# State products and old states' part of y by head, in 64-wide tiles of TensorE's array, in a retention and SwiGLU kernel

## The chip, the cores and the metric

The kernel runs on one core of a Trainium2 chip. The metric is the device time of one execution in microseconds (us), as the median of several executions. A profile is one further look at one execution, with the start and length of each instruction. Its span, from the first to the last instruction, is about 2 us shorter than the time.

TensorE is the matmul engine: an array of 128 rows by 128 columns, which holds the weights (the stationary operand) while the columns of the moving operand stream through. Here it is used as one array or in tiles: two tiles of 64 columns side by side, two of 64 rows, or, in the change, the two tiles of 64 by 64 on the array's diagonal. VectorE, ScalarE and GpSimd work element by element. The profile calls these engines PE, DVE, ACT and POOL, PEld is TensorE's weight loading, and a trailing q (ACTq) marks an engine's sequencer.

## The reference, cut to what matters

```python
# retention: 4 batches, 8 heads, 768 steps, heads of 64
gamma = 1.0 - 2.0 ** (-5.0 - np.arange(H))
for t in range(S):
    state = gamma * state + einsum('bhd,bhe->bhde', k[:, :, t], v[:, :, t])
    y[:, :, t] = scale * einsum('bhd,bhde->bhe', q[:, :, t], state)
# ... y reshaped to x, 3072 tokens by 512, then the SwiGLU FFN
g = x @ w_gate;  val = x @ w_val
out = (g * sigmoid(g) * val) @ w_out
```

## The kernel before

Retention is done in chunks of 128 steps. For a chunk, "scores" multiplies k by q for each head, "mix" adds to y what the states of earlier chunks give and then what the chunk itself gives, and "state" updates the states. There are 8 heads of 64, so two heads fill the 128 partitions: a state tile holds four pairs of heads, and for each pair a block of 128 by 128 in which only the two diagonal 64 by 64 blocks are not zero. The zeros let one full-array matmul serve two heads.

```python
states = [consts.tile([P, NP, P], F32, name=f"state{i}") for i in range(4)]
for t in states:
    nc.gpsimd.memset(t, 0.0)
# ...
def state(c):
    # ... new[:, n] = old[:, n] * gdec, on ScalarE
    st = bank("st")
    for n in range(NP):
        nc.tensor.matmul(st[:, ts(n, P)], kd[:, ts(n, P)], vn[:, ts(n, P)], ...)
    for i in range(2):
        r = ds(D * i, D)
        if ci == 0:
            nc.scalar.copy(new[r, :, r], pairs(st)[r, :, r])
        else:
            nc.vector.tensor_tensor(new[r, :, r], new[r, :, r],
                                    pairs(st)[r, :, r], op=ALU.add)

def mix(c):
    # ...
    y = bank("y")
    if ci:
        prev = state_of(c, 1)
        for n in range(NP):                       # the old states' part
            nc.tensor.matmul(y[:, ts(n, P)], prev[:, n], qd[:, n], ...)
    for n in range(NP):                           # the part within the chunk
        for i in range(2):
            nc.tensor.matmul(y[ds(D * i, D), ts(n, P)], vn[:, ts(2 * n + i, D)],
                             a[i][:, n], ...)
    nc.scalar.copy(xT[:, :, c // NCK % 2, ts(ci % L, P)], pairs(y))
# ... in between: sums for the FFN, its weights' conversion on VectorE
# (tensor_scalar twice, then a merge of the signs) and GpSimd
```

The 24 chunks are spread over four segments of six. The first segment's retention is the start of the kernel, up to 42 us. The other three stand in between the matmuls of an FFN's second product, one or two retention blocks at a time; I call these the three retention stages. The FFN's first product follows each of them. The first one, right after the start, is the "up stage", and TensorE's matmuls of 384 columns belong to it.

Of the kernel before, what the change touches and what calls it, by code (L numbers as in the profile page):

```python
# [10 lines left out]
F32 = mybir.dt.float32  # L11
# [3 lines left out]
ALU = mybir.AluOpType  # L15

P = 128
B, H, S, D = 4, 8, 768, 64
NP = H // 2
# [22 lines left out]
def tile_retnet_swiglu(  # L42
# [37 lines left out]
    nc = tc.nc  # L80

    consts = ctx.enter_context(tc.tile_pool(name="consts", bufs=1))
# [16 lines left out]
    def bank(tag):  # L99

        own = {"x": (0, 1), "wz": (2, 3), "s": (4, 5), "st": (6,), "y": (7,)}[tag]
        turn[tag] = turn.get(tag, -1) + 1
        return banks[own[turn[tag] % len(own)]]
# [200 lines left out]
    gdec = tab[:, GDEC0:NTAB]  # L304



    states = [consts.tile([P, NP, P], F32, name=f"state{i}") for i in range(4)]
    for t in states:
        nc.gpsimd.memset(t, 0.0)  # L310
    xT = consts.tile([P, NC, 2, TH], F32, name="xT")
    xsa = consts.tile([P, 4, KH, TH], F32, name="xs")
    xs = [xsa[:, i] for i in range(4)]
# [5 lines left out]
    def pairs(t):  # L319
        return t.rearrange("p (n t) -> p n t", n=NP)  # L320

    def state_of(c, old=0):
        return states[2 * (c // NCK % 2) + (c + old) % 2]
# [24 lines left out]
    def state(c):  # L348
        ci = c % NCK
        if ci == NCK - 1:  # L350
            return
        vn, kd = chunks[c][2:]
        new, old = state_of(c), state_of(c, 1)
        if ci:
            for n in range(NP):
                nc.scalar.activation(new[:, n], old[:, n], AF.Copy,
                                     scale=gdec[:, ds(n, 1)])
        st = bank("st")
        for n in range(NP):
            nc.tensor.matmul(st[:, ts(n, P)], kd[:, ts(n, P)], vn[:, ts(n, P)],  # L360
                             start=(n == 0), stop=True, skip_group_check=True)
        for i in range(2):
            r = ds(D * i, D)
            if ci == 0:
                nc.scalar.copy(new[r, :, r], pairs(st)[r, :, r])
            else:
                nc.vector.tensor_tensor(new[r, :, r], new[r, :, r],
                                        pairs(st)[r, :, r], op=ALU.add)

    def mix(c):  # L370
        ci = c % NCK
        qd, vn = pairs(chunks[c][1]), chunks[c][2]
        a = att.pop(c)
        y = bank("y")
        if ci:
            prev = state_of(c, 1)
            for n in range(NP):
                nc.tensor.matmul(y[:, ts(n, P)], prev[:, n], qd[:, n],  # L378
                                 start=(n == 0), stop=False, skip_group_check=True)
        for n in range(NP):  # L380
            for i in range(2):
                nc.tensor.matmul(y[ds(D * i, D), ts(n, P)], vn[:, ts(2 * n + i, D)],  # L382
                                 a[i][:, n], start=(ci == 0 and n == 0), stop=True,
                                 skip_group_check=True)
        nc.scalar.copy(xT[:, :, c // NCK % 2, ts(ci % L, P)], pairs(y))  # L385

    def retention(s):



        cs = seg_chunks(s)

        def last(n):
            state(cs[n])
            del chunks[cs[n]]
            if s and n + 3 < len(cs):
                load_chunk(cs[n + 3], places_of(n))

        steps = [lambda: scores(cs[0])]
        for n, c in enumerate(cs):  # L400
            if n + 1 < len(cs):
                steps.append(lambda n=n: scores(cs[n + 1]))
            steps.append(lambda c=c: mix(c))
            steps.append(lambda n=n: last(n))
            if n % 2:
                steps.append(lambda n=n: sums_x(n // 2))
        return steps
# [447 lines left out]
```

## Time and profile before

| | before |
|---|---|
| time, median of 3 (range) | 746.63 us (745.86 to 747.22) |
| span of the profile | 744.2 us |
| first segment, to TensorE's second start | 0 to 41.97 us |
| from there to the last matmul of the up stage (384 columns) | 116.02 us |
| three retention stages | 78.07, 77.39 and 77.51 us |
| from the last matmul of 192 columns to the end | 57.46 us |

I measure a stage from the first second-product matmul after the FFN's first product to the next matmul of 192 columns (which only the later first products have). That takes in some FFN work which does not change, but both ends are sharp in the trace.

This view cuts the kernel before into stretches. Its columns are the stretch, its length, then busy time and number of instructions of PE, PEld, DVE, ACT and POOL, the granted TensorE clock, the DMA share and GB/s.

```profile
0.00:42.00 42.00, 29.20 (x277) 24.64 (x277) 26.58 (x41) 21.00 (x41) 18.88 (x20) 0.99 0.91 316
337.33:414.72 77.39, 77.39 (x522) 66.79 (x521) 41.43 (x77) 14.69 (x39) 9.47 (x8) 1.00 0.36 126
```

In the second row TensorE is busy all of the time and VectorE half of it: there only TensorE's own work counts. In the first row TensorE idles for 13 us and no engine is full, so waits decide.

### The profile page before, as it was taken

How to read it: one execution, taken by the hardware profiler on the slowest of the kernel's cores; microseconds unless marked ns; L12 is line 12 of the kernel's file. 1: busy time of each engine (PE TensorE's matmuls, PEld its weight loads, DVE VectorE, ACT ScalarE, POOL GpSimd, SP SyncE). 2: the span in 40 equal slices, each digit the busy share in tenths (PEclk: the TensorE clock that was granted, in tenths of full speed). 3: DMA queues.
4: the chain of work that ended last, by engine and by line, in shares of the span. 5: the costliest groups of instructions: out<-in, count | busy, mean ns of one | idle time of the engine just before them, and what ended most of it. 6: DMA issues, size and time to landing. Idle time of an engine off the chain costs nothing.

```text
span 744.2 us, 11024 instructions
## 1 busy us (share of the span) xinstructions
PE 720.2 (97%) x4196; PEld 625.5 (84%) x4196; DVE 489.1 (66%) x845; ACT 246.7 (33%) x488; POOL 246.2 (33%) x156
## 2 busy tenths in 40 slices
PE   6889999999999999999999999999999999999997
PEld 5745555568888989997888999998888899999886
DVE  2889999997595787877464466757437356567520
ACT  2687777422211333321221224332221133333100
POOL 3533333423100546382210073554310053726000
PEclk9989999999999999999999999999999999999999
DMA  9968886457958667670543256660284155540010
GB/s 318 370 209 261 256 268 212 143 210 250 335 194 337 239 236 260 250 268 29 186 183 128 84 200 207 208 216 29 85 286 144 38 193 203 199 149 1 1 57 29
DMA packets 60821, 139.01 MB, mean 187 GB/s; under 512 B 4576, under 2 KB 27616, under 8 KB 60768
## 3 DMA queue, kind: packets, MB, share of 16 engines
q1 hardware_dynamic: 57312, 132.01, 52.0%
q10 hardware_dynamic: 3456, 6.29, 2.3%
q8 instruction: 33, 0.54, 0.3%
q14 instruction: 20, 0.16, 0.1%
HBM read 101.72 MB, written 36.57 MB: 186 GB/s over the span
## 4 chain that ended last, share of the span: by engine, by line
PE 86%; DVE 6%; issue 3%; ACT 2%; POOL 2%; DMA 1%; ACTq 0%; SPq 0%; DVEq 0%; POOLq 0%
PE bank L550 38%; PE bank L634 25%; PE bank L437 9%; PE bank L643 4%; PE bank L331 3%; PE bank L382 3%; PE bank L378 2%; PE bank L360 2%; POOL ring L265 2%; DVE ring L277 1%; DMA hT<-in_q_t_dram 1%; DVE ring L258 0%; ACT ring L241 0%; DVE xs L420 0%; DVE ring L252 0%
## 5 line engine op out<-in xcount | busy, mean ns | idle before, releaser
L550 PE MATMUL bank<-loadp,ring 128*128 128x192 f32 x720 | 140.6, 327 | 2.8 <-ACT midp L515 2.8
L634 PE MATMUL bank<-wot,hsp 128*128 128x256 f32 x576 | 130.9, 382 | 0.0
L550 PEld LDWEIGHTS bank<-loadp,ring 128*128 128x128 f32 x720 | 120.5, 190 | 4.2 <-ACT midp L515 4.0
L634 PEld LDWEIGHTS bank<-wot,hsp 128*128 128x128 f32 x576 | 107.7, 190 | 15.9 <-issue 0.5
L515 DVE TENSOR_TENSOR iop<-bank,iop 128x384 f32<-128x384 f32 x144 | 79.7, 555 | 56.7 <-PE bank L550 53.6
L550 PE MATMUL bank<-xs,ring 128*128 128x192 f32 x432 | 87.9, 326 | 0.0
L515 POOL TENSOR_TENSOR iop<-hsp,midp 128x768 f32<-128x768 f32 x9 | 16.3, 1816 | 189.3 <-ACT hsp L515 149.4
L585 POOL TENSOR_TENSOR hT<-iop 128x768 f32<-128x768 f32 x36 | 66.5, 1847 | 35.8 <-DVE iop L515 35.8
L515 ACT COPY hsp<-bank 128x384 f32<-128x384 f32 x90 | 42.9, 479 | 99.5 <-PE bank L550 89.8
L550 PEld LDWEIGHTS bank<-xs,ring 128*128 128x128 f32 x432 | 73.2, 190 | 0.0
L437 PE MATMUL bank<-xs,ring 128*128 128x384 f32 x192 | 67.0, 504 | 2.9 <-DVE xs L420 2.9
L550 PE MATMUL bank<-xT,ring 128*128 128x192 f32 x324 | 66.2, 327 | 1.1 <-DVE iop L515 1.1
L634 PE MATMUL bank<-wot,hT 128*128 128x256 f32 x288 | 65.9, 382 | 0.0
L437 PEld LDWEIGHTS bank<-xs,ring 128*128 128x128 f32 x192 | 37.9, 198 | 30.2 <-DVE xs L420 3.5
L634 PEld LDWEIGHTS bank<-wot,hT 128*128 128x128 f32 x288 | 53.8, 190 | 8.2 <-issue 1.4
L515 DVE TENSOR_TENSOR midp<-bank,midp 128x384 f32<-128x384 f32 x72 | 40.0, 555 | 26.3 <-PE bank L550 24.8
L550 PE MATMUL bank<-hsp,ring 128*128 128x192 f32 x288 | 56.8, 327 | 0.0
L550 PEld LDWEIGHTS bank<-xT,ring 128*128 128x128 f32 x324 | 54.8, 190 | 2.3 <-DVE iop L515 2.2
L437 PE MATMUL bank<-xT,ring 128*128 128x384 f32 x144 | 50.6, 491 | 3.2 <-DVE hT L455 3.2
L550 PEld LDWEIGHTS bank<-hsp,ring 128*128 128x128 f32 x288 | 48.4, 190 | 0.5 <-ACT hsp L515 0.5
L437 PEld LDWEIGHTS bank<-xT,ring 128*128 128x128 f32 x144 | 26.5, 190 | 24.4 <-issue 7.8
L385 ACT COPY xT<-bank 128x512 f32<-128x512 f32 x24 | 14.1, 587 | 96.3 <-PE bank L382 96.3
(139 smaller groups left out, 1015.4 us busy)
## 6 DMA issues: line engine op xcount, KB each, us to landing
ring<-unitt SPq DMA_DIRECT2D x50, 896.0 KB, 4.6
unitt<-ring SPq DMA_DIRECT2D x21, 896.0 KB, 4.6
unitb<-ring SPq DMA_DIRECT2D x12, 896.0 KB, 5.9
ring<-unitb SPq DMA_DIRECT2D x21, 512.0 KB, 5.6
out_dram<-iop ACTq DMA_DIRECT2D x24, 256.0 KB, 3.7
loadp<-in_w_val_dram SPq DMA_DIRECT2D x18, 256.0 KB, 5.9
loadp<-in_w_gate_dram SPq DMA_DIRECT2D x9, 512.0 KB, 6.3
midp<-in_w_out_dram SPq DMA_DIRECT2D x12, 256.0 KB, 3.4
```

The lines of the kernel that those rows point to most:

```text
L265: nc.gpsimd.tensor_tensor(d.bitcast(I32), d.bitcast(I32), lo.bitcast(I32), op=ALU.add)
L331: nc.tensor.matmul(sp[i][:, ts(n, P)], kt[r, n], qt[r, n], start=True, stop=True, skip_group_check=True)
L360: nc.tensor.matmul(st[:, ts(n, P)], kd[:, ts(n, P)], vn[:, ts(n, P)], start=(n == 0), stop=True, skip_group_check=True)
L378: nc.tensor.matmul(y[:, ts(n, P)], prev[:, n], qd[:, n], start=(n == 0), stop=False, skip_group_check=True)
L382: nc.tensor.matmul(y[ds(D * i, D), ts(n, P)], vn[:, ts(2 * n + i, D)], a[i][:, n], start=(ci == 0 and n == 0), stop=True, skip_group_check ...
L385: nc.scalar.copy(xT[:, :, c // NCK % 2, ts(ci % L, P)], pairs(y))
L437: nc.tensor.matmul(o, w[:, slot, k], a[:, k], start=(start and k == 0), stop=(stop and k == KH - 1), skip_group_check=True)
L515: events.append((t, len(events), lambda: fn(*args, **kw)))
L550: nc.tensor.matmul(o[:, h], w[:, h, slot], rhs, start=(start and h == 0), stop=True, skip_group_check=True)
L585: by_block(9.5, 13.5, lambda r: pool(to[:, r], u2[:, r], p5[:, r], op=add))
L634: nc.tensor.matmul(o, a[:, k], wot[k][:, slot], start=(start and k == 0), stop=(k == FH - 1), skip_group_check=True)
L643: nc.tensor.matmul(o, a_dn(0, 0, u)[:, k], wot[k][:, B11], start=(k == 0), stop=(k == FH - 1), skip_group_check=True)
```

## The change

The intent: do each head's product in a tile of the array just as large as it needs, and keep no zeros. A state product becomes eight matmuls with 64 columns of weights and 64 moving columns. The old states' part becomes eight matmuls of 64 by 64 on the diagonal of the array. State tiles become half as large, so that one VectorE addition of 128 partitions does what two of 64 did, and the memsets go.

```diff
-    states = [consts.tile([P, NP, P], F32, name=f"state{i}") for i in range(4)]
-    for t in states:
-        nc.gpsimd.memset(t, 0.0)
+    states = [consts.tile([P, NP, D], F32, name=f"state{i}") for i in range(4)]
@@ state
-        st = bank("st")
+        st = bank("st")[:, : NP * D].rearrange("p (n e) -> p n e", n=NP)
         for n in range(NP):
-            nc.tensor.matmul(st[:, ts(n, P)], kd[:, ts(n, P)], vn[:, ts(n, P)], ...)
-        for i in range(2):
-            r = ds(D * i, D)
-            # copy, or: new[r, :, r] += pairs(st)[r, :, r]
+            for i in range(2):
+                h = ts(2 * n + i, D)
+                nc.tensor.matmul(st[ds(D * i, D), n], kd[:, h], vn[:, h], ...)
+        if ci == 0:
+            nc.scalar.copy(new, st)
+        else:
+            nc.vector.tensor_tensor(new, new, st, op=ALU.add)
@@ mix
             for n in range(NP):
-                nc.tensor.matmul(y[:, ts(n, P)], prev[:, n], qd[:, n], ...)
+                for i in range(2):
+                    r = ds(D * i, D)
+                    nc.tensor.matmul(y[r, ts(n, P)], prev[r, n], qd[r, n], ...)
```

## The prediction

> **What bounds the kernel now.** I read, in this order: the page's busy table and chain of waits, the groups of instructions by form, the chain between 337 and 400 us, and the VectorE and GpSimd timelines up to 42 us.
>
> ```profile
> PE 720.2 (97%) x4196; PEld 625.5 (84%) x4196; DVE 489.1 (66%) x845; ACT 246.7 (33%) x488; POOL 246.2 (33%) x156
> PE 86%; DVE 6%; issue 3%; ACT 2%; POOL 2%; DMA 1%; ACTq 0%; SPq 0%; DVEq 0%; POOLq 0%
> ```
>
> TensorE is 86% of the chain. Work taken from VectorE or ScalarE counts only in their 6% and 2% of it, so the question is what the change takes from TensorE, and where VectorE sets the pace.
>
> ```profile
> L360 PE MATMUL bank<-loadp 128*128 128x128 f32 x80 | 11.3, 284 | 0.0
> L378 PE MATMUL bank<-loadp,state 128*128 128x128 f32 x80 | 10.8, 277 | 0.0
> L382 PE MATMUL bank<-midp,loadp 128*64 128x128 f32 x192 | 13.1, 279 | 0.0
> L356 ACT ACTIVATE state<-state,tab 128x128 f32<-128x128 f32 x64 | 20.4, 393 | 0.6 <-ACT iop L687 0.6
> L367 DVE TENSOR_TENSOR state<-state,bank 64x256 f32<-64x256 f32 x32 | 13.3, 417 | 36.5 <-ACT state L356 35.2 <-PE bank L360 1.1
> ```
>
> L360 is the state product, L378 the old states' part of y, L382 the part within the chunk, L331 the scores. One f32 matmul is two records: with the rows for other buffers L360 and L378 have 160 records each, which is 20 chunks of 4 matmuls. L382 (64-column tiles) and L331 (64-row tiles) are tiled already; the change does that to L360 and L378. Duration is no cost here, since records overlap. The chain gives the cost of a block:
>
> ```profile
> 345.57 2.79 PE bank L634 x12
> ...
> 352.23 1.02 PE bank L382 x16
> 353.26 1.09 PE bank L360 x8
> 354.35 2.59 PE bank L634 x12
> ...
> 361.84 0.89 PE bank L360 x8
> 362.73 2.59 PE bank L634 x12
> 365.33 1.09 PE bank L331 x16
> 366.42 1.09 PE bank L378 x8
> 367.51 1.02 PE bank L382 x16
> 368.53 2.79 PE bank L634 x12
> ```
>
> Twelve L634 matmuls (full array) take 2.59 us after a full-array block and 2.79 after a tiled one. L360 takes 0.89 after L634 and 1.09 after L382. So a change of tiling costs 0.20. The single starts in the trace show of what it is made: the first weight load of L360 starts 201 ns after the last start of L382, of which 109 is that record's own stream, so about 93 ns is emptying the array; then the second matmul comes 214 ns after the first, 107 for a weight load that nothing hides and 107 for the stream. Into L382 the second figure is 160, so its 64-column load costs only 53. A change into a 128-column block costs 93+107 = 0.20, into a 64-column block 93+53 = 0.146. Within L382 and L331 two tiles start 7 ns apart and a pair follows every 109 ns; full-array L360 and L378 take 112 per record.
>
> **What the Trainium skill says.** "TensorEngine Tiling (Array Packing)", section Key Properties: changing the tiling mode drains TensorE, and different tiles can load weights and multiply in parallel. The trace agrees with both (93 ns; 7 ns between the two of a pair). "TensorE: Matmul & The Clock Gate", section LDWEIGHTS: a weight load takes columns / 1.2 ns whatever the rows, so 107 and 53 ns; agreed. The same page, Back-to-back issue gap, gives matmuls of up to 64 columns a floor of about 25 ns, or about 62 ns where decoding is the bound; L382 already issues 16 matmuls in 0.87 us, 55 ns each, so the 62 does not bind here. The tiling page, Gotcha 1, says that different row tiles cannot access the same PSUM bank simultaneously; no pair in this trace does so (L331 writes two banks, L382 has one row group), so it stays a rival.
>
> **The change part by part.**
>
> State product: 4 full matmuls become 8 of 128x64 weights with 64 moving columns, two column tiles side by side. Eight pairs of records instead of eight records. A pair streams 64 columns: half of 107 is 53, and with the 2 to 5 ns that other forms show above their stream I estimate 58. Own time 8 x 0.058 = 0.46 instead of 0.89: minus 0.43.
>
> Old states' part of y: 4 matmuls become 8 of 64x64 on the diagonal of the array. Each still streams 128 columns. Two side by side make eight pairs of 109 ns, 0.87 instead of 0.89: minus 0.02. The halved work does not show: before, the zeros rode along free.
>
> Changes of tiling: before, L360 and L378 had the same tiling as the FFN matmuls between which they stand; now they differ. Per group between two L634 blocks, from the orders that the chain shows (Q the old states' part, C the within-chunk part, S the state product, R the scores):
> - S alone: before 0, now 0.146+0.20 = +0.35.
> - Q C: before 0.146+0.20, now 0.146+0.146+0.20 = +0.15.
> - Q C S: before 0.146+0.20, now 0.146+0.146+0+0.20 = +0.15.
> - C S: before 0.146+0.20, now the same: 0.
> - S R: +0.15. R Q C: before 0.20+0.20+0.146+0.20, now Q's load is short: -0.05.
>
> The stage of 337 to 400 us has six state products, four Q, and the groups R, R, C S, R C, S, R Q C, S R, Q C S, R, Q C S, Q C, S. Own time 6x0.43 + 4x0.02 = 2.66 less; changes 0.35-0.05+0.15+0.15+0.15+0.15+0.35 = 1.22 more (rounded terms): minus 1.44 us. The stages from 160 and from 512 us have four state products and six Q: own time 4x0.43 + 6x0.02 = 1.84 less; groups Q C S twice, R Q C twice, S, S R, Q C twice: 0.97 more: minus 0.87 each. The same sums for before give 73.12 and 77.24 us where the trace has 73.19 and 77.39, so waits on other engines are 0.2 us at most there. Together minus 3.2 us, all on the path.
>
> VectorE and ScalarE: 32 adds of 64 partitions become 16 of 128 (0.42 each, so 6.7 us less busy), 8 copies become 4, the 64 scalings have half the columns, 4 memsets go. All this is hidden behind TensorE except in the first 42 us:
>
> ```profile
> 31.50 0.84 DVE L367 TENSOR_TENSOR state<-state,bank 64x256 f32<-64x256 f32 x2
> ...
> 35.48 0.84 DVE L367 TENSOR_TENSOR state<-state,bank 64x256 f32<-64x256 f32 x2
> ...
> 39.01 0.84 DVE L367 TENSOR_TENSOR state<-state,bank 64x256 f32<-64x256 f32 x2
> 39.88 2.03 DVE L420 TENSOR_TENSOR xs<-xT 128x256 f32<-128x256 f32 x1
> ```
>
> ```profile
> 39.23 2.40 POOL L265 TENSOR_TENSOR ring<-ring,loadp 128x1024 int32<-128x1024 int32 x1 [6.52 <-ACT wot L241]
> ```
>
> TensorE's second start, at 41.97, waits for L420. L420 took 2.03 us instead of 0.42: it ended 0.28 us after L265 of GpSimd. L278, L279 and the earlier L420 also end 0.28 us after a GpSimd instruction, so VectorE's SBUF additions stand still until GpSimd's ends. Up to 28.5 us a transfer of q sets the pace (L331 waits for its landing), so nothing moves there. Of the three 0.42 us saved after it, the first is lost (that L420 still waits for GpSimd's 31.26 to 32.71), the last too (L420 waits for L265), and the middle one moves L265 only as far as ScalarE, its named releaser, lets it. I take minus 0.3. From there the up stage is a loop of TensorE, ScalarE, VectorE and GpSimd that shifts as a whole.
>
> Sum: -3.2 - 0.3 = -3.5; 746.6 - 3.5 = 743.1 us, 0.5% less.
>
> **The rivals.**
> - The naive hope: both groups halve, 40 blocks of 0.89 to 0.45, minus 18 us, 729. Against it: Q streams as many columns as before, and nothing of the added changes is counted.
> - Small pairs at 109 instead of 58, by some floor per matmul or by weight loads one after the other. Then the state product gains 0.02 and only the added changes remain: +0.77, +1.02, +0.77 in the three stages, so 746.6 + 2.6 - 0.3 = 748.9. Against it: loads of a pair start 7 ns apart in L382, and after a semaphore at 28.47 us the sequencer went past 32 instructions in 165 ns, 5 ns each, where 14.5 would be needed.
> - The diagonal tiles share bank 7 and run one after the other: Q takes 1.75 instead of 0.87. With that the stages give +4.4, +2.1, +4.4, less 0.3: 757. Against it: they write different partitions, as L382's do.
> - The start gains all three additions, 1.26 us: 742.1. Or the clock: TensorE was at half speed from 41.3 to 48.1 us in this run, after some 3 us of idleness. A different idle stretch could spare up to 3 us: 740. The idle stretch hardly changes, so I give this little.
>
> **Range and chances.** I hold the main line for some 70%, slow small pairs (or pairs between 58 and 109) for 20%, serial diagonal tiles for 6%. Runs of before differ by 1.4 us. Eight in ten: 741 to 748. Within 2% (731.7 to 761.6) nearly surely: faster 1%, slower 2%.
>
> **What would show it.** State blocks after L382 of 0.46 in the chain, alone 0.61 with the next L634 block at 2.79; Q blocks of about 1.02; the three stages shorter by 0.9, 1.4 and 0.9; TensorE's second start about 0.3 earlier. Wrong if state blocks stay near 0.9, Q blocks reach 1.8, or the difference sits outside these three stages and the start.

## The result, and the profile after

| | runs | median (range), us | ratio to before, 95% interval |
|---|---|---|---|
| before | 6 | 746.67 (745.86 to 747.22) | |
| after | 6 | 742.92 (742.34 to 743.30) | 0.9949 (0.9936 to 0.9962) |

A ratio is the mean time of one kernel's fast runs over that of the other's of the same rounds, so it is not quite the ratio of the medians. The changed kernel is 0.5% faster, and 743.1 was predicted. Its result is correct.

The page of the kernel after, busy times and then the chain of waits:

```profile
PE 712.9 (96%) x4516; PEld 614.0 (83%) x4516; DVE 482.6 (65%) x829; ACT 241.8 (33%) x484; POOL 244.5 (33%) x152
PE 82%; DVE 7%; issue 4%; POOL 2%; DMA 2%; ACT 2%; ACTq 0%; SPq 0%; DVEq 0%; POOLq 0%
```

TensorE has 320 records more and is busy for 7.3 us less, while the span fell from 744.2 to 740.6. So busy time fell twice as much as the span: a record's length counts even where another record overlaps it. VectorE, too, is busy for 6.5 us less, and most of that bought nothing.

The groups by form of the kernel after (line, engine, operation, output from inputs, tile, elements, count | busy us, mean ns | idle before, releaser). L359 is the state product, L376 the old states' part, L364 the state's addition:

```profile
L359 PE MATMUL bank<-loadp 128*64 128x64 f32 x160 | 6.5, 224 | 0.0
L376 PE MATMUL bank<-loadp,state 64*64 64x128 f32 x160 | 10.9, 275 | 0.0
L364 DVE TENSOR_TENSOR state<-state,bank 128x256 f32<-128x256 f32 x16 | 6.7, 418 | 35.8 <-ACT state L353 35.3 <-PE bank L359 0.5
```

The first two rows, like those of the two products that the prediction shows of before, hold half of their line's records; the rest stand in rows for other buffers. In them the state product's busy time fell from 11.3 to 6.5 us, and that of the old states' part stayed (10.8 and 10.9). The addition of 128 partitions takes 418 ns, what one of 64 partitions took.

The same stage as the prediction shows of before, 335 to 400 us, in the chain of the kernel after (start, us, what). L632 is the FFN's second product, L380 the part within the chunk, L328 the scores:

```profile
347.52 2.79 PE bank L632 x12
350.30 1.02 PE bank L380 x16
351.33 0.46 PE bank L359 x16
351.79 2.79 PE bank L632 x12
...
359.48 0.61 PE bank L359 x16
360.10 2.79 PE bank L632 x12
362.88 1.09 PE bank L328 x16
363.98 1.02 PE bank L376 x16
365.00 1.02 PE bank L380 x16
366.02 2.79 PE bank L632 x12
```

Compare with before: a state product after L380 takes 0.46 where it took 1.09, but the L632 block behind it now takes 2.79 where it took 2.59. Standing alone between L632 blocks, it takes 0.61 where it took 0.89, and again L632 pays 0.20: the lone state product gained only 0.08. The old states' part takes 1.02 behind the scores (1.09 before).

The stretch of that stage in the view by stretches, to be held against the second row shown of before:

```profile
335.40:411.39 75.99, 75.99 (x603) 63.72 (x601) 39.59 (x73) 13.00 (x37) 9.49 (x8) 1.00 0.37 129
```

It is 1.40 us shorter, and TensorE is still busy throughout. All the places where the two spans differ, from landmarks in the two profiles:

| | predicted | before | after | difference, us |
|---|---|---|---|---|
| TensorE's second start | -0.3 | 41.97 | 41.37 | -0.60 |
| second start to last matmul of 384 columns | 0 | 116.02 | 115.54 | -0.48 |
| retention stages | -0.87, -1.44, -0.87 | 78.07, 77.39, 77.51 | 77.24, 75.99, 76.68 | -0.83, -1.40, -0.83 |
| the rest between the stages and the end | 0 | 295.49 | 295.47 | -0.02 |
| last matmul of 192 columns to the end | 0 | 57.46 | 57.96 | +0.50 |

These add up to -3.66; the spans differ by 3.65. The three stages are as predicted. The start gave twice its share, and two differences of half a microsecond, which nearly cancel, are in no part of the prediction. The -0.60 is of one pair of profiles, and TensorE's second start moves with the landing of q: in a second profile of the changed kernel (the eighth experiment) it came at 42.31. Counted from the end of VectorE's L279 sum, a fixed place within each profile, it comes 9.72 us later in both profiles of the changed kernel and 10.39 in the one of before: 0.67 us less.

The start, VectorE's timeline and then GpSimd's in the kernel after:

```profile
38.43 0.41 DVE L364 TENSOR_TENSOR state<-state,bank 128x256 f32<-128x256 f32 x1
38.75 2.56 DVE L418 TENSOR_TENSOR xs<-xT 128x256 f32<-128x256 f32 x1
```

```profile
38.64 2.39 POOL L265 TENSOR_TENSOR ring<-ring,loadp 128x1024 int32<-128x1024 int32 x1 [5.85 <-ACT state L353]
```

As before, the VectorE sum that TensorE waits for (L418) ends 0.28 us after GpSimd's L265: 41.31 against 41.03. The Trainium skill, page "SBUF — State Buffer", section Who interferes with whom, says that a VectorE instruction with two SBUF inputs and a GpSimd instruction that reads SBUF exclude each other for the whole instruction; this agrees. So what counts is when L265 starts: at 38.64, 0.59 earlier than before.

The up stage. VectorE at the third weight conversion of the kernel before, then of the kernel after:

```profile
46.91 0.69 DVE L255 TENSOR_SCALAR ring<-ring 128x1024 uint32<-128x1024 uint32 x1
48.14 1.29 DVE L258 SCALAR_TENSOR_TENSOR ring<-bank,ring 128x512 uint32<-128x512 uint32 x2 [0.54 <-ACT iop L470]
```

```profile
46.33 0.69 DVE L255 TENSOR_SCALAR ring<-ring 128x1024 uint32<-128x1024 uint32 x1
47.12 1.29 DVE L258 SCALAR_TENSOR_TENSOR ring<-bank,ring 128x512 uint32<-128x512 uint32 x2
```

Before, VectorE idles for 0.54 us ahead of L258; after, it doesn't. The releaser that the profile names there differs between the runs with this gap (ACT at three lines, DVE at one), so it is hardly what VectorE waited for. Counted from 0 with its sequencer's records, L258 is VectorE's instruction number 63 before. Number 191, 128 further on, is L258 once more, at 113.96 us, with 0.47 us of idleness before it:

```profile
113.96 0.69 DVE L258 SCALAR_TENSOR_TENSOR wot<-bank,wot 128x512 uint32<-128x512 uint32 x1 [0.47 <-DVE wot L255]
```

The end. ScalarE's two issues of the last output, in the kernel before and then after:

```profile
740.55 0.82 ACTq L691 DMA_DIRECT2D out_dram<-iop  x2
```

```profile
736.39 1.05 ACTq L689 DMA_DIRECT2D out_dram<-iop  x2
```

The second issue starts 0.43 us after the first in the kernel before, 0.71 us after it in the kernel after. It is ScalarE's number 703 there, and 703 is 63 + 5 x 128. The list of transfers for the last 4 us of the kernel after also has a packet of instructions, which that stretch of before has not:

```profile
q14 instruction: 1, 0.01, 0.7%
```

### The profile page after: what moved, and what is told of

Read it like the earlier page. It is cut to its first block, busy times and chain, and to the rows that moved or that the text cites. A ratio compares the mean times of both kernels' runs of the same rounds, so it can differ in the third digit from the quotient of the medians.

```text
span 740.6 us, 11633 instructions
## 1 busy us (share of the span) xinstructions
PE 712.9 (96%) x4516; PEld 614.0 (83%) x4516; DVE 482.6 (65%) x829; ACT 241.8 (33%) x484; POOL 244.5 (33%) x152
## 4 chain that ended last, share of the span: by engine, by line
PE 82%; DVE 7%; issue 4%; POOL 2%; DMA 2%; ACT 2%; ACTq 0%; SPq 0%; DVEq 0%; POOLq 0%
PE bank L548 38%; PE bank L632 25%; PE bank L435 6%; PE bank L641 4%; PE bank L328 3%; PE bank L380 3%; PE bank L376 2%; POOL ring L265 2%; DVE ring L277 2%; PE bank L359 1%; DMA hT<-in_q_t_dram 1%; DMA hT<-in_k_t_dram 1%; DMA tab<-in_decays_dram 1%; DVE ring L252 1%; DVE xs L418 0%
## 5 line engine op out<-in xcount | busy, mean ns | idle before, releaser
L632 PE MATMUL bank<-wot,hsp 128*128 128x256 f32 x576 | 131.5, 383 | 0.0
L632 PEld LDWEIGHTS bank<-wot,hsp 128*128 128x128 f32 x576 | 107.6, 190 | 16.3 <-issue 0.5
L632 PE MATMUL bank<-wot,hT 128*128 128x256 f32 x288 | 66.3, 383 | 0.0
L632 PEld LDWEIGHTS bank<-wot,hT 128*128 128x128 f32 x288 | 53.7, 190 | 8.5 <-issue 1.4
```

The lines of the kernel that those rows point to most:

```text
L632: nc.tensor.matmul(o, a[:, k], wot[k][:, slot], start=(start and k == 0), stop=(k == FH - 1), skip_group_check=True)
```

## The experiments

The theory on the three stages is the prediction's: own time 0.46 for a state product, nothing saved by the old states' part, and 0.146 or 0.20 us for every change of tiling. Its rivals are slow small pairs and diagonal tiles that run one after the other. Later a second theory was needed, of the start, the up stage and the end. "Stages" below are the three differences to before. All twelve kernels gave the reference's result, and each is compared with the runs of before (medians 746.4 to 746.7).

**One part alone: the state product.** The kernel before with tiled state products that write into the diagonal blocks of its zero-filled states.

```diff
-            nc.tensor.matmul(st[:, ts(n, P)], kd[:, ts(n, P)], vn[:, ts(n, P)], ...)
+            for i in range(2):
+                r, h = ds(D * i, D), ts(2 * n + i, D)
+                nc.tensor.matmul(pairs(st)[r, n, r], kd[:, h], vn[:, h], ...)
```

> The state product alone by head in 64-column tiles; states keep their zero blocks, the old states' part of y stays a full-array product, the evacuation stays two adds of 64 partitions. Theory (time = own stream of each block plus 0.20 us for each change into a 128-column block and 0.146 into a 64-column one): the three stages with retention beside the second FFN product shorten by 1.2, 1.7 and 1.2 us, 4.2 in all, the start of the up stage hardly moves, about 742.4 us, a shade faster than the whole change (742.9). Rival A (the gain of the whole change is VectorE and ScalarE work that went): nothing left, about 746.5. Rival B (both halved products gain alike): about half of the whole change's 3.8, 744.8.

Measured: 742.81 us (5 runs), ratio 0.9950 (0.9938 to 0.9963); stages -1.21, -1.72, -1.22. The theory's numbers hold, those of both rivals don't. A pair of the small matmuls follows every 58 ns. This one part is worth as much as the whole change.

**The other part alone: the old states' part.**

```diff
-                nc.tensor.matmul(y[:, ts(n, P)], prev[:, n], qd[:, n], ...)
+                for i in range(2):
+                    r = ds(D * i, D)
+                    nc.tensor.matmul(y[r, ts(n, P)], prev[r, n, r], qd[r, n], ...)
```

> The old states' part of y alone by head on the diagonal in 64x64 tiles; the state product stays full, states keep their zero blocks. Theory: own time is unchanged (0.87 for 0.89) and each group that begins with it pays one more change of tiling: the three stages lengthen by 0.36, 0.30 and 0.36 us, 1.0 in all, about 747.7 us. Rival B (both halved products gain alike): 744.8. Rival C (it costs nothing either way): 746.7.

Measured: 747.37 us (5 runs), ratio 1.0013 (0.9999 to 1.0027); stages +0.39, +0.33, +0.38. The chain of this kernel; L380 is the old states' part and L384 the part within the chunk:

```profile
376.32 1.02 PE bank L380 x16
377.35 1.02 PE bank L384 x16
```

In the kernel before the first of these two took 0.89 behind a full-array block. The second is 1.02 in both: a change from 64 by 64 tiles to 128 by 64 tiles costs as much as one from the full array. The diagonal tiles run side by side (1.02, not 1.8), so the rival of serial tiles falls too. In the stages this half of the change is a small loss; the times alone do not tell it from nothing, as the interval includes 1.

**Two additions again.** The changed kernel with the addition in two halves of 64 partitions, to take the saving of VectorE away.

```diff
-            nc.vector.tensor_tensor(new, new, st, op=ALU.add)
+            for i in range(2):
+                r = ds(D * i, D)
+                nc.vector.tensor_tensor(new[r], new[r], st[r], op=ALU.add)
```

> The whole change, but the sum of the states is again two adds of 64 partitions instead of one of 128. Theory: the three stages stay as in the whole change (3.1 us less than before), because VectorE waits for TensorE there; only TensorE's restart after the retention of the start comes some 0.5 us later than in the whole change (41.4): about 743.4 us. Rival A (the gain is VectorE and ScalarE work that went): 16 x 0.42 us come back, 6.7 us, or at least most of the 3.8: 746 or more.

Measured: 744.63 us (5 runs), ratio 0.9974 (0.9962 to 0.9987); stages -0.83, -1.40, -0.83, exactly those of the whole change. So the additions cost nothing in the stages. But 1.2 us more than expected were lost, which asked for a second theory.

**The old states' part in column tiles.** The first experiment's kernel, with the old states' part in the same tiling as the part within the chunk: 128 rows (zeros included) by 64 columns.

```diff
-                nc.tensor.matmul(y[:, ts(n, P)], prev[:, n], qd[:, n], ...)
+                for i in range(2):
+                    r = ds(D * i, D)
+                    nc.tensor.matmul(y[r, ts(n, P)], prev[:, n, r], qd[:, n], ...)
```

> The state product by head as in the whole change, but states keep their zero blocks and the old states' part of y uses 128x64 column tiles with all 128 rows, the same tiling as the two products that follow it. Theory: its own time stays 0.87, and the change of tiling between it and the next block (0.15 to 0.20) disappears: the stages shorten by 1.75, 2.0 and 1.75 us against the kernel before, 5.5 in all, about 741.1 us, 1.8 less than the whole change although twice as many array rows are used. Rival D (64x64 tiles are quicker because they use a quarter of the array): slower than the whole change, 743.5 or more.

Measured: 740.85 us (5 runs), ratio 0.9928 (0.9916 to 0.9941); stages -1.71, -2.00, -1.72. In its chain L382 is the old states' part and L386 the part within the chunk:

```profile
364.42 1.02 PE bank L382 x16
365.45 0.87 PE bank L386 x16
```

L386 takes 0.87 instead of 1.02: the 0.146 of the change is gone. Multiplying zeros in the right tiling beats leaving them out in another.

**Fewer changes.** The changed kernel, with a chunk's blocks put together between FFN blocks (old states, within-chunk, state, next scores), so that no state product stands alone.

```diff
+        if s:
+            def group(n, c):
+                mix(c)
+                last(n)
+                if n + 1 < len(cs):
+                    scores(cs[n + 1])
+                if n % 2:
+                    sums_x(n // 2)
+            return [lambda: scores(cs[0])] + [
+                lambda n=n, c=c: group(n, c) for n, c in enumerate(cs)]
@@ between the FFN's blocks
-            retain((k > 2) + (4 < k < 13))
+            retain(k in (3, 4, 6, 8, 10, 12, 14, 16, 17, 18))
```

> The whole change, with the retention that lies beside the second FFN product reordered: per chunk one group of old states' part, within-chunk part, state product and the next scores, instead of two or three groups spread over as many steps. Same instructions, fewer changes of tiling. Theory: switching in the three stages falls from 5.44, 5.50 and 5.44 us to 4.35, 4.06 and 4.35; about 3.6 us less than the whole change, 739.3 us. Rival (switches hide behind something, or the order matters by waits on VectorE): same as the whole change or slower.

Measured: 739.50 us (4 runs), ratio 0.9907 (0.9892 to 0.9922); stages -1.92, -2.84, -1.92. As the sums of changes gave it.

**Both.** The same grouping on the column-tiled kernel.

> The same grouping on the version with 128x64 column tiles for the old states' part (three neighbouring blocks in one tiling). Theory: switching in the three stages is 3.48 us each, so they shorten by 2.8, 3.5 and 2.8 us against the kernel before, 9.2 in all: about 737.2 us, the fastest of all. Rival: 740.9, as without grouping.

Measured: 738.20 us (4 runs), ratio 0.9891 (0.9878 to 0.9905); stages -2.81, -3.43, -2.81. The stages are as expected; the time is 1.0 above. In its profile a transfer of q landed at 20.8 us, where it landed at 18.4 to 19.8 in the others, and the up stage ended 2.4 us later than before's; that run was also the slowest of the four (739.28). Landing times vary from run to run, so I put no number on the start of single profiles.

**Two additions at the start only.** The third experiment's edit, for the chunks of the first segment alone.

```diff
-            nc.vector.tensor_tensor(new, new, st, op=ALU.add)
+            for r in ([ds(0, D), ds(D, D)] if c in first_chunks else [ds(0, P)]):
+                nc.vector.tensor_tensor(new[r], new[r], st[r], op=ALU.add)
```

> The whole change, with the sum of the states as two adds of 64 partitions only for the six chunks of the start (four sums), one add elsewhere. Theory: VectorE counts only in the start, so the time is that of the run with two adds everywhere, about 744.6 us (1.7 over the whole change). Rival: the later adds made that difference, then 743.3 or less.

Measured: 744.35 us (5 runs), ratio 0.9971 (0.9959 to 0.9984), like the third experiment. So all of the loss comes from four additions in the first 42 us.

**The whole change again,** unedited, on the same chip, as the partner of the last one.

> The whole change again, on the same chip as the three others: 742.9 us, 0.3 either way. If it is 744 or more, the difference of the run with two adds was the chip or the start's clock and not the adds.

Measured: 742.83 us (5 runs), ratio 0.9952 (0.9939 to 0.9964). Against it, the two additions at the start cost 1.5 us. Of that the profiles show 0.67 between the end of the L279 sum and TensorE's second start. The kernels with two additions there have 10.39 to 10.41 us (before and the experiments numbered 1, 2, 3, 4 and 7 in this order), those with one have 9.72 to 9.74 (after, the fifth and this one). A further 0.82 lies between the second start and the last matmul of 384 columns, 116.32 against 115.50. Less is given back elsewhere: the end is 0.47 shorter with two additions, the last stretch of 192-column matmuls 0.23 longer. In the up stage the kernels with two additions have the idleness of VectorE before its third L258, those with one have not.

That gave the second theory: VectorE stands still for about half a microsecond at fixed places in its stream of instructions, 128 apart, and which instruction it strikes is shifted by adding or taking some. Before has the additions' extra instructions ahead of it and is struck at L258; after, with fewer, number 63 is one that waits behind a running instruction. The rival is that the saved time itself lets VectorE catch up. Three runs count instructions without changing the work.

**The whole change and four tiny instructions,** VectorE memsets of one column at the very beginning, which bring number 63 back to where it was.

```diff
+    pad = consts.tile([P, 4], F32, name="pad")
+    for i in range(4):
+        nc.vector.memset(pad[:, ds(i, 1)], 0.0)
     xT = consts.tile([P, NC, 2, TH], F32, name="xT")
```

> The whole change plus four one-column VectorE memsets before its first real work, while VectorE still waits for the first scores: the instruction count up to the first blocks of the up stage is then that of the runs with two adds. Theory (position): VectorE stands still some 0.5 us between its 63rd and 64th instruction, whatever they are; with the count restored this falls again just before the third sign merge, which starts 0.53 us late as in every run with two adds, and the first waits of the up stage end 0.4 us later: restart of TensorE after VectorE's last start-stage work still 9.7 us, but about 743.2 us in all. Rival (the adds themselves, or ScalarE as the named releaser, make that wait): no gap there, 742.8.

Measured: 744.26 us (5 runs), ratio 0.9965 (0.9951 to 0.9978). The idleness of 0.54 us before L258 came back, at 48.70, and the second one at 114.48. The first of them:

```profile
48.70 1.29 DVE L258 SCALAR_TENSOR_TENSOR ring<-bank,ring 128x512 uint32<-128x512 uint32 x2 [0.54 <-ACT iop L471]
```

The time is 1.1 us above the expected 743.2. The up stage takes 116.30 us, 0.79 longer than in the whole change again, where 0.4 was expected; the expectation counted only the first of the two standstills. The profile also has a late transfer of q (19.8 us), and the rest is not settled.

**Before and two tiny instructions,** which move number 63 to L255, ahead of L258.

> The kernel before plus two such memsets and nothing else. Theory (position): the standstill falls between two long instructions of VectorE, behind one that still runs, and is hidden: the gap of 0.53 us before the third sign merge goes, about 0.4 us faster than before, 746.2. Rival: two instructions more can only cost: 746.7 or a little above.

Measured: 745.49 us (6 runs), ratio 0.9988 (0.9976 to 1.0001). VectorE in this run:

```profile
47.06 0.69 DVE L255 TENSOR_SCALAR ring<-ring 128x1024 uint32<-128x1024 uint32 x1
47.86 1.29 DVE L258 SCALAR_TENSOR_TENSOR ring<-bank,ring 128x512 uint32<-128x512 uint32 x2
```

The gap is gone without any work saved, and the up stage takes 115.19 us instead of 116.02. That contradicts the rival in the trace; the interval of the times just touches 1. The clock is not the reason: this profile has no stretch of half clock at TensorE's second start, but neither has that of the sixth experiment, whose up stage takes 116.01 us.

**The grouped, column-tiled kernel and two tiny instructions.**

> The grouped version with column tiles plus two such memsets. Theory: 0.4 us less than without, 737.8. Rival: 738.2 or a little above.

Measured: 736.99 us (735.96 to 737.43, 4 runs), ratio 0.9871 (0.9857 to 0.9884): the best version, 1.3% under before and 0.8% under the changed kernel. It is 1.2 us under the grouped kernel without them, which ran on another chip; in the up stage the traces show 0.86 (115.15 for 116.01). In its chain L385 is the old states' part, L389 the part within the chunk, L365 the state product, L334 the scores, L652 the FFN:

```profile
361.37 1.02 PE bank L385 x16
362.39 0.87 PE bank L389 x16
363.27 0.46 PE bank L365 x16
363.73 1.09 PE bank L334 x16
364.82 5.38 PE bank L652 x24
```

A chunk's whole retention now pays for three changes of tiling (into L385, into L334, and into L652), and two FFN blocks follow without a break (5.38 us for 24 matmuls).

**The end.** The half microsecond at the end looked like the same standstill on ScalarE. It is there in all three profiles that have the changed kernel's ScalarE stream (57.94 to 57.96 us: after, and the eighth and ninth experiments). Two other kernels fit. In the fifth experiment ScalarE has one record less: its number 703 is the closing record behind the last issue, 0.28 us late, and the tail is 57.75 us. In the kernel before, number 703 is an issue of the pair of outputs before the last one, and starts 0.32 us after the wait ahead of it (0.04 at the neighbours), where it holds nothing up. The last run puts four tiny copies into ScalarE's 10 us of idleness before its last copy.

```diff
         nc.scalar.copy(u2, x)
+        if s == NSEG - 1 and u == L - 1:
+            for i in range(4):
+                nc.scalar.copy(pad[:, ds(i, 1)], u2[:, ds(i, 1)])
```

> The whole change, with four one-column copies of ScalarE put into its 10 us of idleness before the last tile's last copy. In the two runs of the whole change and in the one with four more VectorE instructions, the time from the last matmul of 192 columns' block to the end is 57.94 to 57.96 us, against 57.46 or 57.47 in the kernel before and in most others; there ScalarE issues the second output transfer 0.71 us after the first instead of 0.43, and that issue is its instruction number 703, which is 63 and five times 128. Theory (a standstill bound to the place in ScalarE's instruction stream): number 703 now falls into the idle stretch, the two issues stand 0.43 us apart, the tail is 57.46, and the median is 742.4 us, 0.5 below the whole change's 742.9; nothing else in the trace moves. Rival (the tail's 0.5 comes from the output transfers themselves or from the order of the last waits): the tail stays at 57.95 and the median at 742.9.

Measured: 742.80 us (742.10 to 743.52, 5 runs), ratio 0.9952 (0.9938 to 0.9965). ScalarE's issues in this run:

```profile
737.33 0.82 ACTq L693 DMA_DIRECT2D out_dram<-iop  x2
```

The two issues stand 0.43 us apart again, from the last matmul of 192 columns to the end it is 57.46 us, all other stages are as in the changed kernel, and the last packet of instructions is at 728.3 us instead of 738.1. So the trace shows the standstill moved, as the theory had it. The time shows too little: 0.1 of the expected 0.5 us, within the scatter of these runs (1.4 us).

## Why the prediction was right, and where it was not

- **The bound.** TensorE's own work set the time of the three stages before and after, as read from the chain. The hidden work on VectorE and ScalarE was indeed worth nothing there: two additions or one give the same stages to 0.01 us.
- **State product, own time 0.46 for 0.89.** Right: 0.46 to 0.47 after the within-chunk part, 0.61 to 0.62 alone, a pair every 58 ns.
- **Old states' part, 0.02 saved.** Right: 1.02 in every place, a pair every 109 ns. Alone it even loses time.
- **Changes of tiling, 0.20 into 128-column blocks and 0.146 into 64-column ones.** Right: stages -0.83, -1.40, -0.83 for -0.87, -1.44, -0.87. The five other kernels with other blocks or orders (experiments 1, 2, 4, 5 and 6) came out within 0.1 us per stage. Each stage is some 0.04 us off, which I didn't follow. One reading was not exact: pairs within the scores (L331) follow every 112 ns, as full-array records do, and not every 109; no term rests on it.
- **The start, -0.3.** This term was mis-sized: it measured -0.60, or -0.67 within the profiles. The step that failed is "the middle one moves L265 only as far as ScalarE, its named releaser, lets it". L265 starts 0.13 us after the end of VectorE's L258 in both kernels (39.10 to 39.23; 38.51 to 38.64), and the 0.13 is the same in all fourteen profiles, so it waited for VectorE, and all of L258's shift reached TensorE. The saving per addition was also more than 0.42: the next instruction starts 0.87 us after the first of two additions, but 0.33 us after a single one.
- **"The up stage ... shifts as a whole".** This failed. It got 0.48 us shorter, because standstills of VectorE moved behind other work. The runs with tiny instructions put the two of them at about 0.8 us together (0.79 put back, 0.83 and 0.86 taken away). So the changed kernel's up stage is otherwise some 0.3 us longer (115.53 against 115.19 without the standstills, 116.30 against 116.02 with them), which no run here explains.
- **The end.** The prediction has no term for it. A standstill of ScalarE moved into the issue of the last output, for +0.50.
- **The rivals** all fell: slow small pairs and serial diagonal tiles by the chain, the naive 729 by the old states' part and the changes of tiling. A start that gains all three additions, or a lucky clock window, did not show; the fifth experiment had no stretch of half clock at TensorE's second start, and its up stage is that of after to 0.02 us.

So the total, -3.5 for -3.7, is partly luck: -0.3 missing at the start, -0.48 and +0.50 unforeseen that cancel. The part argued from TensorE's blocks, 3.2 us of it, was earned.

What stays open is the standstills' cause. That those named follow the count of instructions is shown in the traces, on two engines, by the four runs with tiny instructions. That there is one at every 128th instruction is not shown: at VectorE's number 319, for one, the kernel before has a gap of 13 ns, behind an instruction of 0.41 us that could hide it. That fetching instructions is the cause is inferred: they lie 128 instructions apart, one of the two instruction queues (q14) moves packets of 8192 bytes, and in the kernels before and after one such packet follows about 1 to 3 us after each of the standstills named. The counts fit as well: in the kernel before q14 moved 20 packets for the 2533 records of VectorE, ScalarE, GpSimd and SyncE, 127 each, and the other queue (q8) 33 packets of 16384 bytes for TensorE's 8491, 257 each. The Trainium skill, page "Runtime: NRT & Kernel Launch", section Instruction fetch mechanics, describes a FIFO that is refilled during execution in 16 KiB blocks of 256 instructions, at a cost mostly hidden; by its ratio, 8192 bytes would be 128 instructions (an estimate). This trace agrees with it in the size of q8's packets, not of q14's, and not in the cost.

## What to carry to other kernels

Before splitting a matmul into tiles, write down the tiling of the blocks before and after it: here a change cost 0.15 to 0.20 us, against 0.46 for a whole tiled state product, so that a part which halved in arithmetic gained nothing, and putting blocks of one tiling together gained about as much again as the change itself (3.6 us in the stages on top of 3.1). What counted here was the moving columns, and not the size of the weights: a pair of tiles took 109 ns with 128 of them, whether it used 128 or 64 rows, and 58 ns with 64. When a difference of about half a microsecond turns up where the work is the same, look whether the count of instructions moved an idle gap that keeps its place in the engine's stream, before believing the releaser that the profile names.

## What the Trainium skill lacked or had wrong

- "TensorEngine Tiling (Array Packing)", Key Properties, says that a change of the tiling mode drains TensorE, but has no figure. Here it took 93 ns and then a weight load that nothing hides: 0.20 us into blocks with 128 columns of weights, 0.146 into those with 64. Two kinds of tiles (64 by 64, then 128 by 64) count as a change as much as the full array does.
- The same page, Gotcha 1, says that different row tiles cannot access the same PSUM bank simultaneously. Tiles on the diagonal, which have different rows and columns, wrote to one bank 6 to 7 ns apart, a pair every 109 ns, with correct results: they write different partitions. So that sentence is broader than what holds here.
- "Runtime: NRT & Kernel Launch", Instruction fetch mechanics, has blocks of 256 instructions and calls their cost mostly hidden. Here the packets of one instruction queue (q8) are 16384 bytes, as it says, but those of the other (q14) 8192. If the standstills are fetches, which is inferred, the cost is not always hidden: those that nothing hid lie 128 instructions apart and held VectorE for 0.47 to 0.54 us and an issue of ScalarE back by 0.28 us.
